# Transposing transfers in place of TensorE transposes for the first batch, with a new table of wanted times

## The chip, the cores and the metric

The kernel runs on one core of one Trainium2 chip. The metric is the device time of one execution in microseconds (us), taken as the median of several runs. The kernel before took 290.94 us (three runs, 290.71 to 290.95).

TensorE (PE in the profile; PEld is its weight load) multiplies matrices into PSUM, which has eight banks here. VectorE (DVE), ScalarE (ACT) and GpSimd (POOL) do elementwise work. Transfers are issued from the queues of SyncE (SP), POOL and ACT and run on 16 DMA engines. Each engine executes its own instructions in the order in which they were written; across engines an instruction waits on semaphores.

## The reference

Sort-net attention, followed by a Fourier mixing layer and an MLP, for 4 batches of 768 rows with 8 heads of 64:

```python
def _attn_ref(q, k, v, sort_net):
    ...                       # P: five rounds of row and column normalisation of exp(sort_net)
    k_sorted = np.einsum('bhij,bhjcd->bhicd', P, k_b).reshape(B, H, S, D)
    v_sorted = np.einsum('bhij,bhjcd->bhicd', P, v_b).reshape(B, H, S, D)
    ...                       # softmax attention inside blocks of 96 rows
    return np.matmul(attn, v_sb).reshape(B, H, S, D).astype(np.float32)

def _moe_ref(x, w_ch1, w_ch2):
    X = np.fft.fft(x, axis=1)
    X = np.fft.fft(X, axis=2)
    mixed = np.real(X).astype(np.float32)
    u = x + mixed
    mu = np.mean(u, axis=-1, keepdims=True)
    var = np.mean((u - mu) ** 2, axis=-1, keepdims=True)
    un = (u - mu) / np.sqrt(var + 1e-06)
    ch = np.maximum(un @ w_ch1, 0.0) @ w_ch2
    return (u + ch).astype(np.float32)
```

## The kernel before

**Stages.** Per batch `b`, `mix` multiplies k and v by the sort matrix (`k_mix`, L821; `v_mix`, L761, whose results DVE adds into the tile `vo`, L772, and `v_move` spreads to `vs` in twelve transfers from SP, L783). `q_mix` (L800) turns q. A step `psQK` is both L800 and L821 of one pair of heads. For each of four pairs of heads and two halves, `maxima` writes scores (`psS`, L853, 16 products for both halves of a pair) and DVE reduces them (`max`, L863); `scores` (`psT`, L875 then L853) gives the scores less their maxima to an exponential on ACT (L880), `minus_one` (L922 on ACT, L924 on DVE) writes the tile `eT`, and `values` (`psN`, L937) makes the attention output, which DVE normalises into `xr` (L943, L944). Batches 0 and 1 take this path; batches 2 and 3 a turned one (`turned`, L892 to L913). Then follow the sequence transform (`fold`, `dft_s`: L983, L995, L999, L1005), the feature transform (`dft_d`: L1035, L1039, L1045, whose results DVE combines as `PQ`, L1058), the residual (L1088; for batch 0 DVE adds in L1100 and L1101), the statistics (`stats`, L1115 and L1116), `root` (ACT, L1124 and L1125), `nm` (DVE, L1128) and `normal`, which writes a tile of normalised rows `un` [128 rows x 512] on ACT (L1138) or DVE (L1141). There are two `un` buffers.

**The turn.** `transpose_u` puts the tile `un[b, i, m]` into `unT` with features on the partitions. For batches 1 to 3 it is one transposing transfer from the SP queue (L1153). For batch 0 it is four TensorE transposes into a PSUM bank (L1162) and a copy from the bank to `unT` on ACT or DVE (L547). There are six such tiles in a batch, three to a group: group 0 is (i, m) = (0,0), (0,1), (1,1), group 1 the others. `mlp(b, gr)` multiplies a whole group: 64 products of L1180 (`ph`) into ACT's `relu` (L1186), then 48 products of L1198 (`pc`) and the output (L1207, stores L1215 and L1219).

**The order.** Engine queues are not written by hand. The class `Plan` holds every step with its possible engines and nominal durations, walks a nominal time line when the kernel is built, and at each turn emits the step that could start first; of those within `NEAR` ns of the first it takes the one with the lowest priority number. That number comes from the nominal length of what hangs on the step, plus `LEAD[name][b]` and `MOVE[name][(b, k)]` in thousands; `REL` gives earliest times for loads. `fill` puts unread products (L687, here called fills) into planned gaps of TensorE of at least 250 ns before `FILL_END`, as long as the planned activity in a window of 3413 ns is under `FILL_LOW`. So a new table rearranges all engines, also where no line of computation was edited.

## Time and profile before

| what | value |
|---|---|
| median of three runs | 290.94 us |
| the profiled execution | 291.53 us, of which the span from the first to the last instruction is 289.7 us |
| mean granted TensorE clock | 0.985 of full speed |
| TensorE transposes of batch 0 (L1162) | 24 products, first at 54.34 us |
| copies to `unT` on ACT (L547) | 6, mean 585 ns |
| transposing transfers of `un` (L1153) | 18, first at 108.0 us |
| fills (L687) | 8 |

Busy time is the time in which an engine had an instruction under way; the granted clock says how fast TensorE was allowed to run in a slice. A bracket at the end of a timeline row is the idle time before the instruction and what ended it. In the view of the chain each piece is what the next one waited for.

### The profile page before, as it was taken

How to read it: one execution, taken by the hardware profiler on the slowest of the kernel's cores; microseconds unless marked ns; L12 is line 12 of the kernel's file. 1: busy time of each engine (PE TensorE's matmuls, PEld its weight loads, DVE VectorE, ACT ScalarE, POOL GpSimd, SP SyncE). 2: the span in 40 equal slices, each digit the busy share in tenths (PEclk: the TensorE clock that was granted, in tenths of full speed). 3: DMA queues.
4: the chain of work that ended last, by engine and by line, in shares of the span. 5: the costliest groups of instructions: out<-in, count | busy, mean ns of one | idle time of the engine just before them, and what ended most of it. 6: DMA issues, size and time to landing. Idle time of an engine off the chain costs nothing.

```text
span 289.7 us, 6877 instructions
## 1 busy us (share of the span) xinstructions
PE 276.1 (95%) x2598; PEld 161.9 (56%) x2598; DVE 191.5 (66%) x435; ACT 183.8 (63%) x455; POOL 122.0 (42%) x190
## 2 busy tenths in 40 slices
PE   7899999689999999999999999999999999999993
PEld 2467766257765565445555576455645645645541
DVE  6749988978797897673679998987866572001011
ACT  2368976778894779746495679788725832712700
POOL 8473736314226789765833256230023641112010
PEclk9979999979999999999999999999999999999998
DMA  7998969998856876969935862553311025002002
GB/s 101 182 162 169 154 106 163 185 140 136 107 88 104 112 147 96 124 143 186 130 88 113 154 112 38 115 144 75 70 38 38 36 54 129 36 34 77 1 36 74
DMA packets 50847, 30.41 MB, mean 105 GB/s; under 512 B 25962, under 2 KB 48900, under 8 KB 50812
## 3 DMA queue, kind: packets, MB, share of 16 engines
q0 software_dynamic: 19040, 19.40, 40.6%
q1 hardware_dynamic: 31574, 10.28, 18.9%
q8 instruction: 20, 0.33, 0.5%
q10 hardware_dynamic: 200, 0.30, 0.4%
q14 instruction: 13, 0.11, 0.2%
HBM read 28.50 MB, written 6.29 MB: 120 GB/s over the span
## 4 chain that ended last, share of the span: by engine, by line
PE 78%; DVE 14%; DMA 3%; issue 2%; ACT 1%; DVEq 0%
PE bank L1180 29%; PE bank L1198 24%; PE bank L983 3%; PE bank L853 3%; PE bank L937 3%; DMA eT<-es 2%; PE bank L1088 2%; PE bank L875 2%; PE bank L821 2%; PE bank L761 2%; PE bank L1005 1%; PE bank L800 1%; DVE st L1115 1%; PE bank L1045 1%; DVE mxs L863 1%
## 5 line engine op out<-in xcount | busy, mean ns | idle before, releaser
L1198 PE MATMUL bank<-w2sb,hr 128*128 128x512 f16 x384 | 90.0, 379 | 0.0
L1180 PE MATMUL bank<-unT,w1sb 128*128 128x384 f16 x512 | 89.2, 329 | 0.0
L1186 ACT ACTIVATE hr<-bank 128x384 f16<-128x384 f32 x128 | 60.7, 495 | 38.7 <-PE bank L1180 37.9
L1180 PEld LDWEIGHTS <-w1sb 128*128 128x128 f16 x512 | 49.1, 99 | 32.2 <-issue 1.5
L1219 POOL DMA_INDIRECT out_dram<-outt,idx_sb x22 | 22.6, 1026 | 88.5 <-DVE outt L1207 70.0
L1198 PEld LDWEIGHTS <-hr 128*128 128x128 f16 x384 | 36.0, 98 | 38.2
L1207 DVE SCALAR_TENSOR_TENSOR outt<-u,bank 128x512 f32<-128x512 f32 x24 | 16.4, 682 | 41.8 <-PE bank L1198 41.8
L892 ACT ACTIVATE sm<-bank,mns 96x96 f32<-96x96 f32 x128 | 32.3, 352 | 2.4 <-DVE mns L898 2.0
L944 DVE TENSOR_TENSOR xr<-bank,rz 96x512 f16<-96x512 f32 x32 | 22.0, 686 | 1.1
L547 ACT CAST W<-bank 128x384 f16<-128x384 f32 (+1 forms) x38 | 12.8, 380 | 12.9 <-PE bank L983 8.5
L1115 DVE BATCH_NORM_STATS2 st<-u 128x6 f32<-128x512 f32 x24 | 16.4, 681 | 4.0 <-POOL u L1101 3.9
L863 DVE TENSOR_REDUCE mxs<-bank 96x8 f16<-96x768 f32 x16 | 14.5, 949 | 5.6 <-PE bank L853 5.5
L1100 POOL TENSOR_TENSOR u<-u,PQ 128x257 f32<-128x257 f32 x18 | 12.8, 711 | 9.9 <-DVE PQ L1058 8.6
L898 DVE TENSOR_REDUCE mns<-bank 96x8 f32<-96x768 f32 x16 | 15.0, 944 | 2.6 <-PE bank L853 2.2
L1101 POOL TENSOR_TENSOR u<-u,PQ 128x255 f32<-128x255 f32 x18 | 12.6, 699 | 3.6 <-DVE PQ L1058 3.6
L908 ACT ACTIVATE es<-sm 96x384 f16<-96x384 f32 x19 | 10.0, 528 | 6.1 <-DMA eT<-es 5.8
L880 ACT ACTIVATE sm<-bank 96x768 f32<-96x768 f32 x16 | 12.8, 801 | 1.4 <-PE bank L853 1.2
L922 ACT ACTIVATE eT<-sm 96x768 f16<-96x768 f32 x16 | 13.4, 841 | 0.4
L569 POOL DMA_DIRECT2D k<-in_k_dram x15 | 11.0, 733 | 5.9 <-PE bank L821 4.8
L937 PEld LDWEIGHTS <-eT 97*128 97x128 f16 (+1 forms) x256 | 11.2, 101 | 3.8 <-ACT eT L922 0.5
L943 DVE RECIPROCAL rz<-bank 96x8 f32<-96x8 f32 x32 | 6.3, 197 | 10.6 <-PE bank L937 10.5
L983 PE MATMUL bank<-cso_sb,xso 120*128 120x384 f16 (+1 forms) x64 | 13.1, 326 | 0.0
(144 smaller groups left out, 426.5 us busy)
## 6 DMA issues: line engine op xcount, KB each, us to landing
vs<-vo SPq DMA_DIRECT2D x48, 65.0 KB
v<-in_v_dram POOLq DMA_DIRECT2D x16, 192.0 KB, 4.9
k<-in_k_dram POOLq DMA_DIRECT2D x15, 192.0 KB, 5.5
q<-in_q_dram POOLq DMA_DIRECT2D x15, 192.0 KB, 4.1
w1sb<-in_moe_w_ch_dram POOLq DMA_DIRECT2D x4, 512.0 KB, 8.0
w2sb<-in_moe_w_ch_dram POOLq DMA_DIRECT2D x4, 512.0 KB, 5.9
eT<-es SPq DMA_TRANSPOSE x32
cdh_sb<-cdh SPq DMA_DIRECT2D x1, 387.0 KB
```

Source lines behind the costliest of these rows:

```text
L863: ("max", b, {"V": 945}, lambda e: nc.vector.tensor_reduce(mxs[n].t.rearrange("p (t j) -> p t j", t=2), pair(pS, BLK), axis=AX.X, op=ALU.max),
L892: nc.scalar.activation(sm.t[:, i], pair(pS, BLK)[:, t, i % 4], AF.Exp, bias=mn.t[:, i:i + 1], scale=-1.0)
L898: ("max", b, {"V": 945}, lambda e: nc.vector.tensor_reduce(mn.t.rearrange("p (t j) -> p t j", t=2), pair(pS, BLK), axis=AX.X, op=ALU.min), ...
L937: nc.tensor.matmul(ps[0:wide(i).stop - BLK * i, i // 4, i % 4], et[0:97, wide(i)], vs[b % 2][:, 4 * y + i % 4, (D + 1) * h:(D + 1) * (h + 1)])
L944: nc.vector.tensor_tensor(xr2[b % 2][0:BLK, 4 * y:4 * y + 4, 128 * hp:128 * hp + 128].rearrange("p j (t d) -> p t j d", t=2), ps[:, :, :, ...
L983: nc.tensor.matmul(ps, x[0:n, j], cso[0:n, j, :], start=(j == 0), stop=(j == 3))
L1115: nc.vector.bn_stats(st.t, us[b, i, m].t)
L1180: nc.tensor.matmul(ps, w1sb[:, mc, 128 * fc:128 * fc + 128], unT[b, gr].t[:, mc, :], start=(mc == 0), stop=(mc == 3))
L1186: nc.scalar.activation(dst, bank(pH, [128, 384]), AF.Relu)
L1198: nc.tensor.matmul(ps, hr[f4].t[:, fc % 4, 128 * t:128 * (t + 1)], w2sb[:, fc, :], start=(fc == 0), stop=(fc == 15))
L1207: step("outt", b, {"V": 687}, lambda e, u=u, pC=pC, o=o: nc.vector.scalar_tensor_tensor(o.t, u.t, RSC, bank(pC, [128, DM]), op0=ALU.mult, ...
L1219: step("store", b, {"G": 1050}, lambda e: nc.gpsimd.indirect_dma_start(out=out.rearrange("b s m -> (b s) m"), out_offset=bass.IndirectOffs ...
```

## The change

`transpose_u` takes the transfer for every batch, and the plan has other numbers: `FILL_LOW`, `FILL_END`, `NEAR`, `SPARE`, `REL`, `LEAD` and `MOVE`. In the changed file lines after L253 stand four lower (L1162 has become L1166, L1180 is L1184).

```diff
-    FILL_LOW, FILL_END, WINDOW = 1931, 49895, 3413
-    LAG, PE_TAIL, MARGIN, NEAR = 45.0, 250.0, 120.0, 14.0
+    FILL_LOW, FILL_END, WINDOW = 2169, 68436, 3413
+    LAG, PE_TAIL, MARGIN, NEAR = 45.0, 250.0, 120.0, 10.0
...
-    SPARE = 909
+    SPARE = 1004
...
-        un=(48.6, 33.2, -20.3, -21.5), unT=(0, 62.4, 0, 15.1),
+        un=(69.9, -4.9, 1.3, 0.6),
...
         dst = lambda: unT[b, gr].t[:, :, 128 * t:128 * t + 128]
-        if b:
+        if True:
             step("turn_u", b, {"S": 1310}, lambda e: nc.sync.dma_start(
                 dst(), un[b, i, m].t, transpose=True),
                 r=[un[b, i, m]], w=[(unT[b, gr], t)], work=850, hop=900)
```

What moves, counted from the two programs: the 24 products of L1162 and the six copies are gone, six transposing transfers stand on SP (24 instead of 18), and there are 23 fills instead of 8. Ahead of the first product of L1180, TensorE has three more `psQK` steps of batch 1 (four instead of one), three more `psT` of batch 1 (five instead of two), 48 more products of `psS` (64 instead of 16) and the four products of L713. Between the row of `psN` for the last `eT` of batch 0 and the first `psS` of batch 1 it has two more groups of L983, one more `psQK` and one fill less. On DVE, between the first `max` of batch 1 and the first L1180, there are two more `max` before the first `PQ`, two more adds of `vo` before `un` of tile (1,1), and one `minus_one` (L924), which was on ACT.

TensorE before, the end of the stretch that leads to the first product of the MLP (`kron` and `v16` belong to `v_mix`, `un` is a tile of normalised rows):

```order
L1162 LDWEIGHTS un0_138
L1162 MATMUL bank_65<-ident_153,un0_138 128x128
...
L761 LDWEIGHTS kron1_85
L761 MATMUL bank_65<-v161_77,kron1_85 128x384
L1180 LDWEIGHTS w1sb_185
L1180 MATMUL bank_65<-unT0_140,w1sb_185 128x384
```

TensorE now, the same place (`mxs2_92` is the maximum of a `psT` of batch 1, third pair of heads):

```order
L879 LDWEIGHTS mxs2_92
L879 MATMUL bank_65<-small_sb_149,mxs2_92 128x96
...
L857 LDWEIGHTS kz2_172
L857 MATMUL bank_65<-qT2_88,kz2_172 128x96
L1184 LDWEIGHTS w1sb_185
L1184 MATMUL bank_65<-unT0_140,w1sb_185 128x384
```

Before, the MLP's first product stood behind transposes and a product of `v_mix`; now it stands behind a `psT` that needs a maximum from DVE. In the run of L1184 that follows, 56 products stand without a break, where 8 stood before.

DVE now, the piece that holds the normalised rows of tile (1,1) (`u3_119`) and that maximum:

```order
L776 SCALAR_TENSOR_TENSOR vo_174<-a16_194,bank_65 128x6x64 x4
L1104 TENSOR_TENSOR u5_121<-bank_65,PQ0_114 128x257
L1105 TENSOR_TENSOR u5_121<-bank_65,PQ0_114 128x255
L1119 BN_STATS st2_131<-u5_121 128x6
L1120 BN_AGGR mv2_128<-st2_131 128x2
L1145 TENSOR_SCALAR un1_139<-u3_119,mv1_127,rstd1_133 128x512
L776 SCALAR_TENSOR_TENSOR vo_174<-a16_194,bank_65 128x6x64
L557 TENSOR_SCALAR kz3_173<-bank_65 128x768
L712 CAST amt_191<-bank_65 128x4x16
L713 TENSOR_TENSOR amt_191<-bank_65,amt_191 128x4x8
L867 TENSOR_REDUCE mxs2_92<-bank_65 96x8
```

Before, ACT wrote `un` of tile (1,1) and `kz` of this pair (L549); now both are DVE's, and seven of the eight adds of `vo` and all statistics of the batch stand ahead of them.

SP now, around the six new transfers (`vs1_176` is `vs` of batch 1):

```order
L748 DMA xr1_184<-a16_194 1x16x32
L1157 DMA_TRANSPOSE unT0_140<-un0_138 128x4x128
L1157 DMA_TRANSPOSE unT0_140<-un1_139 128x4x128
L787 DMA vs1_176<-vo_174 16x8x260 x4
L1157 DMA_TRANSPOSE unT0_140<-un1_139 128x4x128
L1157 DMA_TRANSPOSE unT1_141<-un0_138 128x4x128
L787 DMA vs1_176<-vo_174 16x8x260 x5
L1157 DMA_TRANSPOSE unT1_141<-un1_139 128x4x128
L1157 DMA_TRANSPOSE unT1_141<-un0_138 128x4x128
L787 DMA vs1_176<-vo_174 16x8x260 x3
```

Before, twelve transfers of `v_move` stood here in one run and no transposing transfer; now the third turn, the last that group 0 needs, stands behind four of them.

74 lines of the change are left out of this document (39 added, 35 removed).

## The prediction

> **What bounds the kernel now.** I read the page first, for the span and the chain that ended last.
>
> ```profile
> span 289.7 us, 6877 instructions
> ...
> PE 78%; DVE 14%; DMA 3%; issue 2%; ACT 1%; DVEq 0%
> ```
>
> TensorE carries most of the chain, so what counts is when TensorE cannot work and how much work it has left. The view in windows shows where that is (columns: the window, its length, busy time of PE, PEld, DVE, ACT and POOL with their instructions, granted TensorE clock, share of the DMA engines, GB/s).
>
> ```profile
> 50.00:60.00 10.00, 6.13 (x59) 3.69 (x58) 9.61 (x29) 7.02 (x16) 4.04 (x7) 0.96 1.06 161
> 60.00:70.00 10.00, 9.86 (x151) 6.60 (x150) 7.68 (x16) 7.74 (x15) 2.99 (x4) 0.87 0.89 133
> 100.00:110.00 10.00, 9.55 (x112) 5.95 (x111) 9.45 (x18) 8.35 (x24) 8.81 (x16) 1.00 0.83 146
> 120.00:130.00 10.00, 9.43 (x71) 4.61 (x70) 7.13 (x15) 5.16 (x18) 6.47 (x11) 1.00 0.71 141
> 54.80:58.20 3.40, 2.02 (x11) 0.82 (x11) 3.23 (x11) 3.37 (x8) 0.00 (x0) 1.00 1.26 199
> 59.30:62.70 3.40, 3.26 (x16) 1.70 (x14) 3.40 (x10) 2.32 (x4) 0.00 (x0) 0.52 0.83 112
> ```
>
> From 50 to 60 us TensorE is busy for 6.13 of 10 us while DVE is busy for 9.61: there DVE sets the pace. The two later windows that I show, with 9.55 and 9.43, are the only ones between 70 and 280 us that lose more than 0.1 us. So the time is the start of the first MLP product (L1180), plus the work that TensorE then has left, plus little. The narrow windows show that work too: with 2.02 of 3.40 us busy from 54.8 on, the granted clock in the window from 59.3 is 0.52. The chain tells what released the first L1180:
>
> ```profile
> 59.02 0.54 PE bank L1162 x4
> ...
> 60.70 2.27 PE bank L1180 x8
> 62.97 0.45 PE bank L1162 x8
> ```
>
> It started at 60.70 by the chain (60.49 by the timeline, which counts the pipelined start), behind transposes that themselves stood behind DVE.
>
> **The change, part by part.** Three things move: transposes and copies leave; work that stood behind the first L1180 now stands ahead of it; and the first L1180 itself moves.
>
> *Work that TensorE no longer has behind the first L1180.* Prices are differences of starts in the timeline (start, duration, engine, line, what):
>
> ```profile
> 44.65 0.51 PE L875 MATMUL bank<-small_sb,mxs 96*128 96x96 f16 x8
> ...
> 45.37 0.52 PE L875 MATMUL bank<-small_sb,mxs 96*128 96x96 f16 x8
> ...
> 60.49 2.47 PE L1180 MATMUL bank<-unT,w1sb 128*128 128x384 f16 x8
> 62.80 0.61 PE L1162 MATMUL bank<-ident,un 128*128 128x128 f16 x8
> ...
> 63.99 0.53 PE L800 MATMUL bank<-ident,q 128*64 128x128 f16 x12
> ...
> 65.45 0.40 PE L713 MATMUL bank<-ident,amt 128*128 128x128 f16 x4
> 65.69 0.81 PE L1180 MATMUL bank<-unT,w1sb 128*128 128x384 f16 x4
> 66.43 0.53 PE L800 MATMUL bank<-ident,q 128*64 128x128 f16 x12
> ...
> 67.23 0.52 PE L853 MATMUL bank<-kz,qT 64*128 64x96 f16 x16
> 67.67 1.47 PE L1180 MATMUL bank<-unT,w1sb 128*128 128x384 f16 x8
> ...
> 76.52 1.47 PE L1180 MATMUL bank<-unT,w1sb 128*128 128x384 f16 x8
> 77.82 0.51 PE L875 MATMUL bank<-small_sb,mxs 96*128 96x96 f16 x8
> ```
>
> The two transposed tiles behind it cost 0.45 (the chain's piece at 62.97; the other four tiles were ahead). Three psQK: 65.45 - 63.99 = 1.46 for two, 67.23 - 66.43 = 0.80 for the third, 2.26 together. L713: 65.69 - 65.45 = 0.24. Sixteen products of psS: 67.67 - 67.23 = 0.44; 48 are 1.32. A psT: 45.37 - 44.65 = 0.72; three are 2.16. Sum 6.43 us. So the break-even is simple: if the first L1180 starts 6.4 us later than 60.5, at 66.9, the end doesn't move.
>
> *When the first L1180 can start.* It now stands behind a psT that needs the maximum mxs2_92, and DVE has that behind all of the batch's statistics. The DVE rows of before:
>
> ```profile
> 43.46 1.82 DVE L863 TENSOR_REDUCE mxs<-bank 96x8 f16<-96x768 f32 x2 [0.99 <-PE bank L853]
> 45.20 0.75 DVE L1058 TENSOR_TENSOR PQ<-bank,ot 128x258 f32<-128x258 f32 x2
> 46.95 0.43 DVE L1100 TENSOR_TENSOR u<-bank,PQ 128x257 f32<-128x257 f32 x1 [1.00 <-PE bank L1088]
> ...
> 49.02 0.76 DVE L1058 TENSOR_TENSOR PQ<-bank,ot 128x258 f32<-128x258 f32 x2 [0.36 <-ACT ot L547]
> ...
> 58.41 1.49 DVE L772 SCALAR_TENSOR_TENSOR vo<-a,bank 128x384 f16<-128x384 f16 x3
> ...
> 60.81 0.54 DVE L1141 TENSOR_SCALAR un<-u,mv,rstd 128x512 f16<-128x512 f32 x1
> ...
> 62.66 0.22 DVE L708 CAST amt<-bank 128x64 f16<-128x64 f32 x1
> 62.91 0.19 DVE L709 TENSOR_TENSOR amt<-bank,amt 128x32 f16<-128x32 f32 x1
> ```
>
> The anchor is the first max of batch 1, at 43.46. It moves because TensorE has two more groups of L983, one more psQK and one fill less ahead of it:
>
> ```profile
> 42.49 0.65 PE bank L983 x4
> ...
> 48.27 0.65 PE bank L687 x3
> ```
>
> That is 2 x 0.65 + 0.80 - 0.22 = 1.88 at most. Part of it fills waits that TensorE has there, as the fills show: three fills' worth, 0.65, of the 1.88 I leave out and take 1.2; the ends are 0.6, where two thirds would be hidden, and 1.9. Then DVE in order:
>
> - four max instead of two: 45.20 - 43.46 = 1.74 for two, so 3.48;
> - from the first PQ to un, the same PQ, adds, statistics and five vo as before: 60.81 - 45.20 = 15.61, less the idle time in brackets, 1.00 and 0.36, which the two max ahead will cover: 14.25;
> - two more vo: 1.49 / 3 = 0.50 each with the overlap left in, say 0.95;
> - minus_one on DVE, which this trace doesn't have for a whole tile. Half a tile took 0.603 on DVE in the turned batches, and a tile of 128x768 out of PSUM 0.953:
>
> ```profile
> L910 DVE TENSOR_SCALAR es<-sm 96x384 f16<-96x384 f32 x13 | 7.8, 603 | 4.5 <-DMA eT<-es 2.6 <-ACT sm L892 1.5 <-ACT hr L1186 0.4
> ...
> L553 DVE TENSOR_SCALAR kz<-bank 128x768 f16<-128x768 f32 x3 | 2.9, 953 | 1.4 <-PE bank L821 1.4
> ```
>
> So between 0.6 (an operation for half the data) and 1.2 (two of them); I take 0.9, nearest to the row of the same width. ACT, which loses this step, is not waited for here.
>
> The normalised rows of tile (1,1) then start on DVE at 43.46 + 1.2 + 3.48 + 14.25 + 0.95 + 0.9 = 64.2. Two paths go on from there. On DVE: un 0.54, one vo 0.5, kz 0.95, the two small steps of amt 0.22 + 0.19, the max 0.91 (half of 1.82): 3.3, so 67.5; then the psT at 0.72, so 68.3. The other path is the transfer:
>
> ```profile
> 235.72 0.52 DVE L1141 TENSOR_SCALAR un<-u,mv,rstd 128x512 f16<-128x512 f32 x1
> ...
> 237.42 0.54 DVE L1141 TENSOR_SCALAR un<-u,mv,rstd 128x512 f16<-128x512 f32 x1
> ...
> 238.81 0.81 ACT L1138 ACTIVATE un<-u,nm,rstd 128x512 f16<-128x512 f32 x1 [2.44 <-DMA unT<-un]
> ...
> 241.91 0.55 DVE L1141 TENSOR_SCALAR un<-u,mv,rstd 128x512 f16<-128x512 f32 x1 [0.95 <-DMA unT<-un]
> ```
>
> In the last batch un ended at 235.72 + 0.52 = 236.24 and its buffer came free for ACT at 238.81: 2.57 us for a turn. The second, ended at 237.96, freed its buffer at 241.91: 3.95, with others queued ahead. With 2.57 the group is there at 64.2 + 0.5 + 2.6 = 67.3, hidden under the DVE path by 1.0; with 3.95 at 68.7, which would cost 0.4. On SP this turn is queued behind four v_move, whose vo stand on DVE ahead of three more vo and a tile's statistics; behind it wait the other v_move, and their vs is wanted only by psN, which now stands 56 products after the first L1184. POOL issues none of this.
>
> So the first L1180 comes at 68.3, 7.8 us later, against 6.4 us that it leaves behind: **1.4 us slower**. The ends: with 0.6 for the anchor and 0.6 for minus_one it is 67.4 (0.5 slower); with 1.9, 1.2 and the longer turn 64.2 + 0.7 + 0.3 + 0.5 + 3.95 = 69.7 (2.8 slower).
>
> *The fills.* Fifteen more at 0.22 would be 3.3 us, and I cost them at nothing: they stand where TensorE waits for DVE anyway (eight of them around psV and the psQK behind it, which wait for PSUM banks that DVE frees). If DVE were not late, they would be the whole loss.
>
> *The copies.* Six on ACT leave; ACT was not what the first L1180 waits for now, so nothing.
>
> *The clock.* Eight L1180 took 62.80 - 60.49 = 2.31 under the low clock and 77.82 - 76.52 = 1.30 at full speed: 1.0 us is lost today. In the change TensorE is again waiting for DVE between 55 and 68, with 23 fills in all, so I leave this loss as it is. It could vanish (-1.0), or a whole slow window of 3.4 us could fall on the products (1.7 instead of 1.0, +0.7).
>
> The Trainium skill (TensorE: Matmul & The Clock Gate, Part 1, What's actually happening) says that the array falls to half clock after an idle window of about 3.4 us and comes back after a busy one. The trace agrees on the half and on the length (0.52 over 3.4 us), but not on idle: 2.02 of 3.40 busy was not enough. By the rule, fills alone would keep the clock and the sum would be 0.4 us slower; by the row, 1.4.
>
> *Around the rest.* Everything after the first L1180 is re-ordered too, but the end is the same: the last two MLP groups run as whole blocks in both programs. The windows with 9.55 and 9.43 lose 1.0 us together; the new order may lose none of it or as much again. I take no difference, and 1.0 either way for the range.
>
> The profiled execution took 291.53 with a span of 289.7, 1.8 outside. Span 291.1, profiled 292.9; the median of the runs lies 0.59 under that execution, so **292.3**.
>
> **Rivals.**
>
> *The clock and the later stalls pay.* The fills keep the array above what the gate asks for, all 1.0 us comes back, the stream runs clean for another 1.0, and the chain is at its short end: 0.5 - 1.0 - 1.0 = -1.5, 289.4. It decides in favour of faster once the first L1184 starts before 67 with a clock of 1.0 in the window after it. For it: 15 more fills in just that stretch, and DVE is freed of two max, which before stood behind the first L1180. Against it: fills stand at planned gaps, and the wait for psV's banks is where the array is emptiest.
>
> *It balances.* The chain at its short end and half of the clock: 0.5 - 0.5 = 0, 290.9. For it: 7.8 against 6.4 are two big numbers each known to half a microsecond.
>
> *The turn becomes the bound.* The DMA share is 1.26 in the window from 54.8: the third turn, behind transfers of v and weights, takes 3.95 plus as long as an earlier one needs to clear (1.4 more). Then the group lands at 64.2 + 0.5 + 5.4 = 70.1 and with the longer anchor (0.7) at 70.8: 10.3 - 6.4 = 3.9 slower, 294.8. Against it: SP has nothing else queued there. The Trainium skill (VectorE: DVE Perf Modes, The three transpose paths and Rules for kernel authors) speaks for this side: TensorE where PSUM will do as target, 390 ns for 128x128, and 1309 ns by transfer. Its figure for four blocks one after the other would be an estimate of 5.2 us a tile and 3.3 us lost; the row of 2.57 us does not bear that out.
>
> *The change does not do what it says.* Of the 24 transposes 16 stood in a stretch where TensorE waited for DVE. Taking those away gives nothing, in any of the cases; only the 0.45 behind the first L1180 counts, and it is in the sum.
>
> **How the numbers follow.** The forecast, slower by 0.6 to 2.8, has 0.44. The turn as bound, or new stalls of that size, 0.16. Balance 0.15. Faster 0.25. About 0.2% (0.6 us) is what a measurement of this kernel can tell from no change. So faster 0.25, same 0.15, slower 0.60. The forecast's own range is 291.5 to 293.7. To leave out no more than 2 in 10, the range goes down to 290.0, most of the way to the fast case, and up to 294.5, just short of the turn as bound.
>
> **What would show it.** In the profile after: the first L1184 near 68.3, with 67 as the point that decides; DVE without idle from the first max of batch 1 (near 44.7) to mxs2_92; un of tile (1,1) near 64.2 and its turn about 2.6 us behind; TensorE idle or in fills for some 8 us between 54 and 68; the clock under 0.6 in a window that touches the first L1184; fewer than 1.5 us idle from there to the last product. The prediction is wrong in its mechanism if L1184 starts before 66 or is released by the transfer rather than by the psT, and wrong in its balance if the work behind it has not shrunk by 6.4 us.

## The result

| | before | after |
|---|---|---|
| median of the runs | 290.94 us | 300.08 us (298.12 to 301.91, four runs) |
| the profiled execution | 291.53 us, span 289.7 | 298.77 us, span 296.8 |
| mean granted TensorE clock | 0.985 | 0.980 |
| first L1180, now L1184 | 60.49 us | 73.60 us |

The ratio is 1.031 (95% interval 1.024 to 1.038): slower by 9 us, where 1.4 were forecast. Ratios leave out runs that lie far above their kernel's shortest (the profiled executions of e10 and e11 below are two such) and, for the experiments, the profiled execution; medians keep them all, so the two can differ.

The page of the changed kernel, span and chain:

```profile
span 296.8 us, 6876 instructions
...
PE 79%; DVE 8%; DMA 8%; issue 2%; POOL 1%; SPq 1%; ACT 0%; DVEq 0%; POOLq 0%
```

DMA has 8% of the chain, where it had 3%: transfers have become something that TensorE waits for. The chain names two of the pieces (start, length, what):

```profile
28.03 7.64 DMA cse_sb<-cse
...
77.80 5.96 DMA vs<-vo
```

The second is a `v_move` of batch 1, behind the start of the MLP. The first is the load of the constant `cse`, which stands nowhere in the prediction. TensorE's timeline shows what it did:

```profile
35.72 0.99 PE L999 MATMUL bank<-cse_sb,xse 120*128 120x386 f16 x3 [2.37 <-DMA cse_sb<-cse]
37.01 0.32 PE L1003 MATMUL bank<-nse,xse 96*128 96x192 f16 x1 [0.30 <-POOL nse L1337]
...
40.55 0.67 PE L941 MATMUL bank<-vs,eT 97*128 97x65 f16 x8
...
47.48 0.69 PE L857 MATMUL bank<-kz,qT 64*128 64x96 f16 x24
```

L999 and L1003 are the first products of the sequence transform of batch 0, and need `cse` and `nse`, which POOL makes of it. TensorE stood for 2.4 us, and its clock was at half from 35.50 to 42.33. The last `psN` of batch 0 (L941) came at 40.55, where it had been at 38.28:

```profile
38.28 0.43 PE L937 MATMUL bank<-vs,eT 97*128 97x65 f16 x8 [0.39 <-ACT eT L922]
```

The first `psS` of batch 1 followed at 47.48, where it was at 43.08 before. SP's timeline shows that `cse`, issued at 16.86 before, now stands behind eight `v_move` transfers (the last two rows are `v_move` of batch 1 and the turns of group 0's third tile and the next):

```profile
18.42 5.72 SPq L787 DMA_DIRECT2D vs<-vo  x6
...
26.73 1.26 SPq L787 DMA_DIRECT2D vs<-vo  x2
28.03 0.71 SPq L1247 DMA_DIRECT2D cse_sb<-cse  x1
...
66.32 2.55 SPq L787 DMA_DIRECT2D vs<-vo  x4
68.96 2.70 SPq L1157 DMA_TRANSPOSE unT<-un  x2
```

And POOL's shows what ran beside it. Before, the first quarter of `w2` (512 KB) came at 58.51. Now one comes at 26.14, as soon as the quarter of `w1` under way has landed, with k and v behind it:

```profile
25.90 0.18 POOL L497 COPY landed<-w1sb 1x1 f16<-1x1 f16 x1 [8.18 <-DMA w1sb<-in_moe_w_ch_dram]
26.14 0.75 POOL L1240 DMA_DIRECT2D w2sb<-in_moe_w_ch_dram  x1
...
28.95 0.74 POOL L573 DMA_DIRECT2D k<-in_k_dram  x1
29.69 0.72 POOL L563 DMA_DIRECT2D v<-in_v_dram  x1
35.77 1.18 POOL L1337 TENSOR_SCALAR nse<-cse_sb 96x384 f16<-96x384 f16 x1 [5.36 <-DMA cse_sb<-cse]
```

From there the DVE rows follow the forecast closely, and then fall behind once more:

```profile
47.94 3.55 DVE L867 TENSOR_REDUCE mxs<-bank 96x8 f16<-96x768 f32 x4 [1.48 <-PE bank L857]
...
55.05 0.84 DVE L928 TENSOR_SCALAR eT<-sm 96x768 f16<-96x768 f32 x1
...
68.28 0.52 DVE L1145 TENSOR_SCALAR un<-u,mv,rstd 128x512 f16<-128x512 f32 x1
...
69.80 0.96 DVE L557 TENSOR_SCALAR kz<-bank 128x768 f16<-128x768 f32 x1 [0.55 <-PE bank L825]
...
71.03 1.81 DVE L867 TENSOR_REDUCE mxs<-bank 96x8 f16<-96x768 f32 x2
```

The work between the anchor (the first max, 47.94) and `un` of tile (1,1) took 20.3 us. The last stretch, on TensorE:

```profile
66.38 1.89 PE L691 MATMUL bank<-junk 128*128 128x512 f16 x4
...
72.03 0.38 PE L717 MATMUL bank<-ident,amt 128*128 128x128 f16 x4 [0.51 <-DVE mxs L867]
72.25 0.59 PE L691 MATMUL bank<-junk 128*128 128x512 f16 x2
72.89 0.50 PE L879 MATMUL bank<-small_sb,mxs 96*128 96x96 f16 x8
...
73.60 6.67 PE L1184 MATMUL bank<-unT,w1sb 128*128 128x384 f16 x40
```

Four planned fills took 1.9 us at half clock (66.22 to 69.63), and behind the max (71.03) stand the four products of L717 (the step `psB`), two fills and the `psT` before the first L1184.

### The profile page after: what moved, and what is told of

Same layout as the page of the kernel before. It is cut to its first block, busy times and chain, and to the rows that moved or that the text cites. A ratio compares the mean times of both kernels' runs of the same rounds, so it can differ in the third digit from the quotient of the medians.

```text
span 296.8 us, 6876 instructions
## 1 busy us (share of the span) xinstructions
PE 279.9 (94%) x2589; PEld 163.5 (55%) x2589; DVE 188.9 (64%) x439; ACT 182.9 (62%) x445; POOL 121.7 (41%) x190
## 4 chain that ended last, share of the span: by engine, by line
PE 79%; DVE 8%; DMA 8%; issue 2%; POOL 1%; SPq 1%; ACT 0%; DVEq 0%; POOLq 0%
PE bank L1202 26%; PE bank L1184 26%; PE bank L987 3%; PE bank L857 3%; PE bank L1092 3%; DMA cse_sb<-cse 3%; PE bank L804 2%; PE bank L941 2%; DMA vs<-vo 2%; PE bank L825 2%; DMA q<-in_q_dram 2%; PE bank L1049 2%; PE bank L765 2%; PE bank L879 1%; PE bank L691 1%
## 5 line engine op out<-in xcount | busy, mean ns | idle before, releaser
L1202 PE MATMUL bank<-w2sb,hr 128*128 128x512 f16 x384 | 89.0, 379 | 0.0
L1184 PE MATMUL bank<-unT,w1sb 128*128 128x384 f16 x512 | 87.7, 326 | 0.0
L1184 PEld LDWEIGHTS <-w1sb 128*128 128x128 f16 x512 | 48.8, 98 | 32.2 <-issue 0.2
L551 ACT CAST W<-bank 128x384 f16<-128x384 f32 (+1 forms) x32 | 11.3, 388 | 18.2 <-PE bank L1009 7.4
L941 PEld LDWEIGHTS <-eT 97*128 97x128 f16 (+1 forms) x256 | 12.1, 106 | 4.9 <-issue 1.6
L941 PE MATMUL bank<-vs,eT 97*128 97x65 f16 (+1 forms) x256 | 13.2, 202 | 1.2 <-DMA vs<-vo 1.0
L553 ACT ACTIVATE kz<-bank 128x768 f16<-128x768 f32 x13 | 10.2, 812 | 5.4 <-PE bank L825 5.2
L926 ACT ACTIVATE eT<-sm 96x768 f16<-96x768 f32 x15 | 12.5, 842 | 1.3 <-PE bank L941 0.9
L585 POOL TENSOR_TENSOR vh<-v 128x384 f32<-128x384 f16 x12 | 11.2, 930 | 4.2 <-DMA v<-in_v_dram 2.3
```

Source lines behind the costliest of these rows:

```text
L941: nc.tensor.matmul(ps[0:wide(i).stop - BLK * i, i // 4, i % 4], et[0:97, wide(i)], vs[b % 2][:, 4 * y + i % 4, (D + 1) * h:(D + 1) * (h + 1)])
L1184: nc.tensor.matmul(ps, w1sb[:, mc, 128 * fc:128 * fc + 128], unT[b, gr].t[:, mc, :], start=(mc == 0), stop=(mc == 3))
L1202: nc.tensor.matmul(ps, hr[f4].t[:, fc % 4, 128 * t:128 * (t + 1)], w2sb[:, fc, :], start=(fc == 0), stop=(fc == 15))
```

## The experiments

All experiments but two keep every instruction of one of the two kernels, in its order on each engine, except for the pieces shown. The steps are recorded as the planner lays them out and written down at the end with those pieces moved, so lines of the experiments stand some lines lower than those above, and names are what to go by. "psS" is the start of the first `psS` of batch 1, "first MLP" that of the first L1180 or L1184, "half clock" the sum of the windows at half clock ahead of 280 us, all three of the profiled execution. The kernel before, run again beside the experiments, had medians of 291.2 to 292.0 us; ratios go by those runs. `psN`, `psT`, `psB` and `psV` (the products of L761) name TensorE's part of a step.

| run | median us (lowest to highest) | ratio to before (95%) | psS | first MLP | half clock |
|---|---|---|---|---|---|
| before | 290.9 | | 43.08 | 60.49 | 6.8 |
| after | 300.08 (298.1 to 301.9) | 1.031 (1.024 to 1.038) | 47.48 | 73.60 | 10.2 |
| e1, cse early | 298.23 (298.0 to 299.7) | 1.024 (1.016 to 1.032) | 47.62 | 74.21 | 13.7 |
| e3, w2 late | 299.02 (297.0 to 300.9) | 1.027 (1.017 to 1.038) | 46.23 | 72.81 | 6.8 |
| e4, both | 300.36 (297.2 to 301.6) | 1.031 (1.023 to 1.040) | 46.59 | 72.67 | 6.8 |
| e5, before, turn only | 299.05 (296.0 to 299.9) | 1.022 (1.012 to 1.032) | 43.06 | 65.51 | 17.1 |
| e8, cse early, w2 much later | 296.26 (294.9 to 297.6) | 1.013 (1.005 to 1.021) | 47.00 | 73.82 | 10.2 |
| e2, before, cse late | 297.82 (296.5 to 298.6) | 1.019 (1.010 to 1.027) | 48.83 | 66.30 | 17.1 |
| e10, before, w2 early | 294.13 (289.7 to 296.0) | 1.002 (0.996 to 1.009) | 45.25 | 62.42 | 10.2 |
| e9, before, half the turns | 293.62 (291.0 to 298.4) | 1.004 (0.999 to 1.009) | 41.93 | 59.09 | 6.8 |
| e11, after, fills | 298.89 (296.4 to 301.9) | 1.024 (1.016 to 1.031) | 49.60 | 76.97 | 13.7 |
| e15, e2 with fills | 296.04 (294.5 to 297.6) | 1.018 (1.012 to 1.025) | 46.03 | 63.19 | 3.4 |
| e12, e5 with fills | 299.21 (295.4 to 301.1) | 1.030 (1.022 to 1.037) | 41.47 | 65.42 | 3.4 |
| e13, e8 with fills | 296.89 (296.1 to 300.8) | 1.018 (1.013 to 1.022) | 44.44 | 72.74 | 10.2 |
| e16, before, loads beside a turn | 291.80 (290.4 to 293.9) | 1.001 (0.996 to 1.006) | 42.45 | 59.72 | 6.8 |
| e17, e8 and more | 299.54 (297.8 to 300.4) | 1.025 (1.017 to 1.033) | 44.26 | 72.64 | 10.2 |
| e18, after, six fills less | 300.63 (300.0 to 301.3) | 1.029 (1.022 to 1.037) | 48.70 | 74.64 | 20.5 |
| e19, before, short products | 293.38 (291.3 to 295.3) | 1.007 (1.003 to 1.011) | 43.04 | 60.20 | 0 |

### Undoing the new places of cse and w2 (e1, e3, e4)

```diff
 SP, batch 0 (e1, e4):
+DMA cse_sb<-cse
 DMA vs<-vo x6
 DMA xr<-m x3
 DMA vs<-vo x2
-DMA cse_sb<-cse
 DMA vs<-vo x4
 POOL (e3, e4):
-COPY landed<-w1sb
-DMA w2sb<-in_moe_w_ch_dram
 TENSOR_TENSOR kron x2
 DMA k
 DMA v
 TENSOR_SCALAR nse<-cse_sb
+COPY landed<-w1sb
+DMA w2sb<-in_moe_w_ch_dram
```

> The changed kernel, with one instruction moved: the load of cse stands on SP ahead of the v_move transfers of batch 0, as it did before, instead of behind eight of them. Theory A (the late load of cse and the slow clock that the wait brings make the loss beyond the forecast): TensorE no longer waits for cse at 35.7 us, the granted clock stays near 1.0 between 36 and 42 us, the first psS of batch 1 comes at 43 to 44.5 instead of 47.5, the first L1184 3 to 4.5 us earlier than 73.6, and the time falls by 3 to 5 us, to 294 to 297. Rival B (the transposing transfers are what costs): the wait at 35.7 goes, but the time falls by less than 1 us. Rival C (the new order of DVE in batch 1 decides the first L1184): the first psS comes earlier, the first L1184 by less than half of that, and the time falls by 1 to 2 us.

> The changed kernel, with one load moved: the quarter of w2 that POOL issued at 26.1 us (behind a wait for w1) stands behind nse instead. cse is issued where the changed kernel has it, at 28 us. Theory A1 (the load of cse is slow because 512 KB of w2 run beside it, and nse waits behind it on POOL): cse lands in 3 to 4 us instead of 7.6, near 31.5, TensorE hardly waits, and the time falls by 3 to 5 us as in the kernel with the early cse. Theory A2 (being issued at 28 is late enough by itself): cse lands near 34 or later and the time falls by less than 1.5 us. Rival B: less than 1 us whatever cse does.

> The changed kernel with both moves: cse ahead of the v_move transfers and the quarter of w2 behind nse. Theory A: about the time of the kernel with the early cse alone (within 1 us), 294 to 297, since either removes the same wait; still 3 to 6 us slower than before, because the first L1184 stands behind DVE by the rest (68 to 70 us, against 66.9 that would balance). Rival B: 297 to 299.

Theory A missed in all three: 1.9, 1.1 and -0.3 us instead of 3 to 5, and the intervals overlap that of the changed kernel. The wait for `cse` went (in e3 it shrank from 2.4 to 0.6 us), but TensorE's row in e1 shows a new one 1.6 us further on, and e1's chain names it:

```profile
37.36 1.56 PE L956 MATMUL bank<-vs,eT 97*128 97x65 f16 x24 [2.28 <-DMA vs<-vo]
```

```profile
30.33 6.90 DMA vs<-vo
```

The last `v_move` of batch 0, issued at 30.33, landed 6.9 us later, and the first `psS` came no earlier than before the edit. In e4 the same wait took 2.7 us: there `nse` no longer holds POOL up, so `w2` comes at 30 us and does the same harm. In e3 TensorE waited 1.6 us for the load of q instead, which was now behind `w2` on POOL. In these profiles one late transfer hid the next.

### The turn alone (e5)

```diff
-            ps = bank(pY, [128, 4, 128], F16)
-            for c in range(4):
-                nc.tensor.matmul(ps[:, c], un[b, i, m].t[:, 128 * c:128 * (c + 1)], ident, is_transpose=True)
+            nc.sync.dma_start(dst(), un[b, i, m].t, transpose=True)
...
-                   ("unT", b, {"A": 585, "V": 400}, lambda e: copy(
-                       e, dst(), bank(pY, [128, 4, 128], F16)), [pY], [(unT[b, gr], t)]))
+                   ("unT", b, {"A": 585, "V": 400}, lambda e: None, [pY], [(unT[b, gr], t)]))
```

> The kernel before, in its own order, with nothing but the turn changed: the four TensorE transposes and the copy of each of the six tiles of batch 0 are replaced, at the place of the transposes, by a transposing transfer from SP. Theory A (the turn by transfer is about as fast as TensorE with its bank and copy where TensorE waits for DVE anyway): the first L1180 within 0.7 us of 60.5, the time within 1 us of before, 290 to 292. Rival B (the transfers are what costs): each group of the MLP waits 2.6 us or more for its third tile, the time rises by 2 to 5 us, 293 to 296.

Rival B held in kind, and the loss was above its 2 to 5 us: 2.2% slower (299.05 us against 291.85 of the kernel before beside it), with nothing else moved. The rows of the turns on SP, of `un` on ACT and of the first L1180 (here L1188):

```profile
54.30 2.62 SPq L1171 DMA_TRANSPOSE unT<-un  x2
...
62.94 2.60 SPq L1171 DMA_TRANSPOSE unT<-un  x2
```

```profile
53.46 1.52 ACT L1149 ACTIVATE un<-u,nm,rstd 128x512 f16<-128x512 f32 x2 [0.52 <-DVE nm L1139]
...
61.39 1.52 ACT L1149 ACTIVATE un<-u,nm,rstd 128x512 f16<-128x512 f32 x2 [5.51 <-DMA unT<-un]
```

```profile
65.51 4.00 PE L1188 MATMUL bank<-unT,w1sb 128*128 128x384 f16 x12 [6.02 <-DMA unT<-un]
```

The first two tiles were written by 54.98 us and their turns issued from 54.30 on, but the next writers of the two buffers ran only at 61.39: 7 us for turns that I had put at 2.57. The third turn, issued at 62.94, let the MLP start at 65.51, and the first twelve products ran at half clock, which lasted from 54.21 to 71.28. What stood in the way is in the view of the DMA queues (queue, packets, MB, share of 16 engines) for 50 to 58 us:

```profile
q0 software_dynamic: 1696, 1.51, 119.3%
q14 instruction: 1, 0.01, 0.3%
```

q0 carries POOL's loads and q1 SP's transfers. POOL's loads of k and `w1` have a share of over 100%, and of q1 there is not one packet, though SP has issued two turns from 54.30 on and the first of three small transfers at 57.02. In before and after together there are 111 microseconds in which POOL's loads have a share of 1.0 or more; in those SP's queue has a mean share of 0.015 and at most 0.24. That figure doesn't say in how many of them SP had anything to send.

### Both loads out of the way, and the opposite edits on before (e8, e2, e10, e9)

e8 is e1 with the quarter of `w2` moved behind the last loads of q and v for batch 1. e2 puts `cse` and `nse` of the kernel before where the changed one has them, e10 the quarter of `w2`. In e9 only the second group's three tiles are turned by transfers (the edit of e5 behind `if gr:`).

> The changed kernel with two loads moved: cse ahead of the v_move transfers (as in the run with the early cse), and the quarter of w2 that POOL issued at 26.1 us much later on POOL, behind the last loads of q and v for batch 1. Theory S (while POOL's loads fill the DMA engines, a transfer from SP gets next to nothing, so whatever SP sent last before such a load lands late: cse in the changed kernel, v_move in the run with the early cse): the last v_move of batch 0 lands by 34 us instead of 37.2, no idle stretch of TensorE over 1 us between 30 and 44, the first psS of batch 1 at 43.5 to 45 instead of 47.5, the first L1184 near 70.5, and the time falls by 2 to 4 us, to 295 to 297. Rival O (the new order behind the first psS decides, and what is won ahead of it is lost there, as in the three runs before): the first psS comes earlier and the time falls by less than 1 us.

> The kernel before, in its own order, with the load of cse moved to where the changed kernel has it, behind eight v_move transfers, and nse on POOL behind the second load of v. POOL has no load of weights near it here. Theory S (lateness on SP costs nothing by itself, a large POOL load beside it does): cse is issued near 27.5 us, lands within 3.5 us, L995 still starts within 0.7 us of 32.6, and the time is within 0.8 us of before. Rival L (the place behind the v_move transfers is what costs): cse lands after 34 us, TensorE waits 2 us or more, and the time rises by 2 to 4 us.

> The kernel before, in its own order, with one load moved: a quarter of w2 (512 KB) is issued by POOL near 26 us, behind a wait for the quarter of w1 that is under way, where the changed kernel has it, instead of near 66. cse stays early. Theory S: the SP transfers that are under way from 27 to 31 us (v_move, cso) land 3 us or more later than before, TensorE waits 1.5 us or more between 29 and 40, and the time rises by 1.5 to 4 us. Rival L (the load is harmless, only the order on SP counts): the time within 0.7 us of before.

> The kernel before, in its own order, with only the second group of three tiles of batch 0 turned by transfers from SP; the first group keeps TensorE and its copies. Theory S (a turn by transfer costs where the MLP waits for it while loads are under way, and nothing where there is slack): the first L1180 within 0.5 us of 60.5, TensorE has 0.2 to 0.5 us less work behind it, the time between 0.7 us less and 0.7 us more than before. Rival T (the transfers of batch 0 cost by themselves, through SP's queue or the un buffers): 2 us or more slower.

e8 is the one edit that brought the changed kernel back by a measured amount, 3.8 us, inside the range of theory S. But the steps that the theory named did not come in its profile: TensorE still waited 1.2 us for `v_move`, the first `psS` came at 47.00 instead of 43.5 to 45, and the first MLP product no earlier than before the edit. What released that product is no longer the psT:

```profile
36.01 0.93 PE L960 MATMUL bank<-vs,eT 97*128 97x65 f16 x24 [1.21 <-DMA vs<-vo]
...
73.82 1.46 PE L1203 MATMUL bank<-unT,w1sb 128*128 128x384 f16 x8 [0.80 <-DMA unT<-un]
```

It waited 0.80 us for `unT`: the turn was next in line. The profiled execution is the longest of the four, 297.57 us at a mean granted clock of 0.979; the other three ran at 0.991 and 0.992. So where the 3.8 us were won is not shown. e2 went against theory S and for rival L: `cse`, issued at 29.96 us, landed 4 us later, TensorE waited twice (1.5 us for `v_move`, 1.2 ahead of the product that needs `cse`), half clock lasted from 30.63 to 44.28, and the time rose by 5.9 us against the kernel before beside it, though only a load of v (192 KB) was near. POOL's row of `nse` shows the landing:

```profile
33.94 1.18 POOL L1351 TENSOR_SCALAR nse<-cse_sb 96x384 f16<-96x384 f16 x1 [6.40 <-DMA cse_sb<-cse]
```

So standing behind `v_move` costs with a small load near it too; that it would cost with none is not shown.

e10 can't be decided: the profiled execution, which the ratio leaves out, has psS 2.2 us later, and the ratio shows no change. e9 held: where the MLP has slack, a turn by transfer costs nothing that can be measured.

### Is it the clock? (e11, e15, e12, e13)

All kernels showed half clock behind these waits. Four kernels got fills where TensorE only waits.

```diff
 TensorE (e11: x10; e15: x7; e13: none)
+MATMUL bank<-junk
 MATMUL bank<-cse_sb,xse
 TensorE (e15: x5, first psN; e13: x7, fifth psN)
+MATMUL bank<-junk
 MATMUL bank<-vs,eT
 TensorE (e12: x25, x6 and x5 more ahead of it)
+MATMUL bank<-junk
 MATMUL bank<-unT,w1sb
 TensorE, last psQK of batch 1 (e11, e13: x5 more)
+MATMUL bank<-junk
 MATMUL bank<-ident,q
```

> The changed kernel, all its instructions in their order, with fills added where TensorE only waits: ten ahead of the first psWe (the wait for cse, 2.4 us) and five more beside those ahead of the last psQK of batch 1 (a wait of 1.7 us for DVE). Theory G (the waits themselves are the smaller part; a window of 3.4 us in which TensorE is busy for less than about 2.1 us is followed by half clock, and that is the larger part): the wait for cse stays, no window of half clock begins between 34 and 60 us, the first psS of batch 1 comes 1.5 to 3 us earlier than 47.5, and the time falls by 2 to 4 us from 300.1, to 296 to 298. Rival W (the waits are the loss, the clock only follows them): the time falls by less than 1 us, or rises by what the fills cost (up to 3 us).

> The kernel before with the late cse (the run that took 297.8, with TensorE waiting for 3 us in all between 29 and 36 us and 13.7 us of half clock behind it), with five fills ahead of the first psN and seven ahead of the first psWe, where it waits. Theory G: no window of half clock between 28 and 50 us, the time back to 292 to 294.5. Rival W: the time stays at 296.5 to 298.5.

> The kernel before with only the turn changed (the run that took 299.05, with TensorE waiting 6.0 us for the third turn and 17 us of half clock), with fills where it waits: five ahead of L695 of batch 1, six among the places of the old transposes, 25 ahead of the first L1180. Theory G: the first L1180 still comes at 64.5 to 66 us, since the turn is as late as it was, but the clock stays high, and the time falls by 2.5 to 4.5 us, to 294.5 to 296.5; what is left against before, 3 to 5 us, is the wait for the transfer itself. Rival W: the time stays at 298 to 300, or above where the fills overrun the wait.

> The changed kernel with the early cse and the late quarter of w2 (the run that took 296.3), with fills where it still waits: seven ahead of the psN that waits for v_move at 36 us, and five more ahead of the last psQK of batch 1. Theory G: no half clock between 34 and 60 us, at most one window of it between 60 and 72, the first psS at 44 to 45.5 us, the time 293 to 295, which is near the forecast for the change (292.3). Rival W: the time stays at 295.5 to 297.5.

In the profiled executions of e15 and e12 the half clock shrank from 17.1 to 3.4 us, and these two took 294.48 and 295.39 us. The medians moved less: 1.8 us less for e15, 0.2 more for e12, 1.2 less for e11, 0.6 more for e13, against 2 to 5 expected. By the times theory G missed.

Two things keep this from settling what the clock is worth. First, the profiles bear the theory out as far as the first `psS`. e13 has the orders of e8 with fills added: its waiting psN came 0.4 us later (36.43, in e8 36.01), and its first `psS` still 2.6 us earlier (44.44 against 47.00), inside the range of the theory, without the half clock that e8 had from 37.40 to 44.23. e15 has it 2.8 us earlier than e2. What e13 won it lost again: five extra fills came to stand behind the wait that they were meant for, and nine fills took 4 us at half clock. The same five stand there in e11. In e12 the first L1180 stands right behind the last fill, so the wait itself can't be read from it.

Second, half clock differs from one execution of a program to the next. e12's other three ran at mean granted clocks of 0.986, 0.973 and 0.980 instead of 0.994, so the half clock was back in them. e13 took 296.06 us at 0.994 and 299.77 at 0.981, e11 296.39 at 1.00 and 300.08 at 0.980. Of 56 comparable executions of the kernel before, 35 had a clock of 0.99 or more and a mean time of 291.1 us, the others a lower one and 292.5. Whether the clock makes the difference, or a late transfer makes both, is not shown.

### A load beside a turn, and the crossed kernels (e16, e6, e7)

```diff
 POOL, batch 3 (e16):
 TENSOR_TENSOR u<-u,PQ x2
+DMA k<-in_k_dram x3
 DMA out_dram<-outt,idx_sb
```

> The kernel before, in its own order, with three loads of 192 KB from POOL added near 234 us, beside the transposing transfers of the last batch, where no load runs otherwise. They fetch again what the buffers of k already hold, and nothing reads it. The turn of the second tile (from the end of un to the next writer of its buffer) took 2.57 us without them. Theory S (SP's transfers get next to nothing while POOL's loads fill the DMA engines): it takes 4.5 us or more, and the packets of the SP queue come in the gaps of the loads; the time rises by up to 3 us, as far as the first L1180 at 243.5 waits. Rival F (the engines are shared fairly, the late turns of batch 0 have another reason): it takes at most 3.5 us and the time stays within 0.7 us.

> The changed kernel's table of wanted times with the turn of batch 0 still by TensorE, its bank and its copies. The planner lays out its own order for it, which is neither of the two. Theory S (the loss has two parts, the table's places for cse and w2, about 4 us, and the transfers themselves under the loads of that stretch, about as much): 293 to 297. Rival T (only the transfers cost): within 1 us of before. Rival N (the new table is the whole loss): 298 to 301.

> The kernel before with its own table and the turn of batch 0 by transfers; the planner lays out its own order for it. cse stays early and no w2 is near it. Theory S: the turns wait for the loads of w1 and k that POOL sends between 47 and 53 us, the first L1180 comes at 64 us or later, and the time is 295 to 299. Rival N: within 1 us of before.

e16 measured the disputed cost by itself, far from the change. `un` of the second tile and the next writer of its buffer:

```profile
236.84 0.79 DVE L1155 TENSOR_SCALAR un<-u,mv,rstd 128x512 f16<-128x512 f32 x1
...
242.99 0.81 ACT L1152 ACTIVATE un<-u,nm,rstd 128x512 f16<-128x512 f32 x1 [5.49 <-DMA unT<-un]
```

From 237.63 to 242.99: 5.36 us for the turn, 2.57 without the loads. In the view of the queues for 237 to 240 us SP's queue has two packets:

```profile
q0 software_dynamic: 598, 0.43, 111.4%
q1 hardware_dynamic: 2, 0.00, 0.1%
```

Theory S held, and the time didn't move: the next MLP group started at 244.64 without a wait. The crossed kernels say nothing on the parts: 309.96 us (306.5 to 314.0) and 303.25 us (301.9 to 305.6, ratio 1.039, 1.031 to 1.048), both slower than either kernel and outside every expectation. The planner laid out a new order for each mixture, and both orders were worse.

### Everything at once, and the clock on before (e17, e18, e19)

e17 is e8 with seven fills ahead of the waiting psN, 16 and 28 short unread products (128x128) in the waits between the psV of batch 1, and without the six planned fills ahead of the last psQK and of the psT; e18 is the changed kernel without those six; e19 is before with 4 and 20 short products between the psV.

> The changed kernel with all that the runs so far point to: cse early, the quarter of w2 late, seven fills ahead of the psN that waits for v_move, the six planned fills ahead of the last psQK and of the psT before the first L1184 taken out (four of them took 1.9 us at half clock and held up kz), and 44 short unread products in the two waits of TensorE for DVE between the psV of batch 1, written to the free end of their banks. Theory G (late transfers, then half clock, then fills on the path, and nothing else, lie between forecast and result): no half clock between 34 and 72 us, the first psS near 44.5, un of tile (1,1) near 65, the first L1184 at 68.5 to 70 (the forecast was 68.3), the time 292 to 294.5. Rival O (the new order behind the first psS is slow by itself): the first L1184 at 71.5 or later and the time 295.5 or more.

> The changed kernel without the six planned fills ahead of the last psQK and of the psT that stands before the first L1184. Theory P (those fills stood on the path: 1.9 us of them at half clock ahead of kz, 0.4 us ahead of psT): DVE no longer waits for kz, the first L1184 comes 0.8 to 1.5 us earlier after un of tile (1,1) (5.3 us in the changed kernel), and the time falls by 0.5 to 1.5 us from 300.1. Rival N (fills cost nothing, as the prediction has it): the distance from un to the first L1184 within 0.3 us of 5.3 and the time within 0.5 us.

> The kernel before, with 24 short unread products in TensorE's waits between the psV of batch 1 (55 to 59 us, busy for 1.45 of 3.41 us there), written to the free end of their banks. Theory G (half clock follows a window in which TensorE is busy for less than about 2.1 of 3.4 us): the window of half clock at 59.1 goes, eight L1180 take 1.3 to 1.6 us instead of 2.31, and the time falls by 0.3 to 1.2 us against before. Rival W: the clock window stays or the short products hold TensorE up, and the time is within 0.5 us of before or above it.

In e17 the anchor came back: psS at 44.26, the first max at 44.71. The first MLP product still came at 72.64, and time and place are those of rival O. The chain and TensorE's row name the reason, and POOL's row what ran beside it:

```profile
66.54 5.97 DMA unT<-un
```

```profile
72.64 3.68 PE L1228 MATMUL bank<-unT,w1sb 128*128 128x384 f16 x11 [1.43 <-DMA unT<-un]
```

```profile
62.45 0.74 POOL L1284 DMA_DIRECT2D w2sb<-in_moe_w_ch_dram  x1
```

The turn of tile (1,1) was issued at 66.54 behind four `v_move`, and landed 6.0 us later: 512 KB of `w2` filled the engines until 67.5, and SP's queue had the `v_move` to move first. In this order a better anchor does not bring the transfer in before 72.5. From 67.31 to 77.55 the clock was at half as well. e18 shows that the six fills cost nothing on balance: from `un` of tile (1,1) to the first L1184 it took 5.14 us, with them 5.32, and the time didn't fall; rival N held. They were not idle weight, though. The wait for kz went, as theory P had it, but without the fills half clock lasted from 65.12 to 78.77, where it had been 66.22 to 69.63, and TensorE's steps there took longer (the first eight products of the psT 0.80 us instead of 0.50).

In e19's profile the half clock at 59.1 is gone and eight L1180 take 61.49 - 60.20 = 1.29 us, where they took 2.31:

```profile
57.52 1.28 PE L473 MATMUL bank<-junk 128*128 128x128 f16 x20
58.98 0.85 PE L1181 MATMUL bank<-ident,un 128*128 128x128 f16 x8 [0.18 <-DVE vo L791]
...
60.20 1.46 PE L1199 MATMUL bank<-unT,w1sb 128*128 128x384 f16 x8
61.49 0.61 PE L1181 MATMUL bank<-ident,un 128*128 128x128 f16 x8
```

TensorE was 1.2 us ahead there, and by 125.8 us, at a product that waits 0.77 us for ACT, the lead was gone. So in this execution the won window was worth nothing at the end. The time rose by 0.7% (0.3 to 1.1), but that ratio says little on the clock: only the profiled execution ran at 0.997, and the mean of the twelve, 0.990, is that of the kernel before beside it. No version was measurably faster than the kernel before.

## Why the prediction was wrong

The direction was right (slower, 0.60), the time was not: 300.08 lies 5.6 us above the range. By steps, with the last rows of both kernels for the ends of the MLP:

```profile
274.68 10.52 PE L1198 MATMUL bank<-w2sb,hr 128*128 128x512 f16 x48
```

```profile
281.72 10.52 PE L1202 MATMUL bank<-w2sb,hr 128*128 128x512 f16 x48
```

| step | forecast | measured |
|---|---|---|
| work behind the first MLP product | 6.43 less | (285.20 - 60.49) - (292.24 - 73.60) = 6.07 less |
| first max of batch 1 | 44.7 | 47.94 |
| from there to `un` of tile (1,1) | 19.5 | 20.34 |
| from there to the first L1184 | 4.1 | 5.32 |
| span | 291.1 | 296.8 |

- **The balance** was right: 6.07 against 6.43, and the span is longer by the 5.3 us by which the first L1184 is later than forecast, plus 0.4. As a law it isn't: in e13, e17 and e19 a better start of the MLP was lost again behind it.
- **The anchor** is the first step that failed, and the largest, 3.2 of the 5.3 us: "It moves because TensorE has two more groups of L983, one more psQK and one fill less ahead of it". The list of what moved was read on TensorE and DVE, and on SP only around the turns. That `cse` had gone behind eight `v_move` on SP, and a quarter of `w2` ahead of it on POOL, was not priced, nor was a clock that falls ahead of the MLP. In the changed kernel TensorE waited 2.4 us for `cse`, ran at half clock to 42.33, and had the last `psN` of batch 0 at 40.55 instead of 38.28. With both loads moved away and fills in the wait (e13 and e17) the first max is at 44.89 and 44.71, so the sum over TensorE held, at its upper end: in e13 it takes 6.60 us from that `psN` (37.84) to the first `psS`, 1.80 more than before, where 1.88 was the most. With the loads moved and no fills (e8) the max is at 47.46. The 3.2 us are therefore the late transfers and the half clock behind them together, and the profiles do not divide them.
- **The transfer path** is the second: "With 2.57 the group is there at 64.2 + 0.5 + 2.6 = 67.3, hidden under the DVE path by 1.0". The 2.57 came from the last batch, where POOL loads nothing beside that turn. Beside loads a turn took 5.4 (e16), 6.0 (e17) and 7 us (e5). In the changed kernel this is hidden by the late psT; as soon as that comes earlier, the turn decides (e8, e17). The rival "the turn becomes the bound" had the mechanism, with "behind transfers of v and weights" as its cause, and was given a sixth of the chance and 294.8 us; its argument against, "SP has nothing else queued there", looked at the wrong queue.
- **The other rivals**: no start ahead of 67 and no balance came. That taking the transposes away gives nothing but the 0.45 us in the sum fits the balance.
- **The new steps on DVE** were right: four max 3.55 (forecast 3.48), `minus_one` 0.84 (0.9). The 0.84 more up to `un` are waits for TensorE's banks (0.52 and 0.31 for L1092). The 1.2 more behind it are DVE's wait for kz (0.55) and the psB and two fills ahead of the psT.
- **The fills** cost nothing on balance, as forecast, but for another reason than forecast: they held the clock (e18).
- **The clock** was priced at the MLP's products alone. Half clock rose from 6.8 to 10.2 us and lies ahead of the MLP now (full clock from 69.6 on), where it helped to make the anchor late. What a window of it is worth in time stays open. The window that the prediction read, 2.02 us busy from 54.8 on, was off the grid on which the clock changes; on it, 55.71 to 59.12 has 1.45 us busy, and half clock follows at 59.12.
- **Two smaller points.** The 3.3 us in the rival of the turn come out as 3.1 from its own rows. And 0.2% was taken as what a measurement can tell; the intervals here reach 0.4% to 1.0% either way.
- **The median** lies 1.3 us above the profiled execution, where it lay 0.6 below before: 1.9 of the 7.8 us.

What divides the 9 us: the places of `cse` and `w2` are worth 1.8 points of the 3.1% (e8), by the time and not by a row of the profile, and what is left, 1.3%, holds the forecast 0.5% and what else the new order costs, the late turn among it. e2 and e5 alone cost 1.9% and 2.2%, together more than the whole; that late transfers cover one another, as in e1, would explain it, but is not shown for these two. How the last 1.3% divides is not settled: e17, meant to settle it, brought 44 new products with it, had half clock under the first MLP products, and its time was above that of e8.

## What to carry to other kernels

A transfer's duration depends on its place as much as on the transfer: take it from a row with the same other queue loading beside it, and read the packets of each queue in that window before calling a transfer hidden. When an order is laid out anew, list every issue on every queue that changed sides with another, constants and weights too, not only those around the edit. And when undoing one late transfer brings nothing, look for the next one behind it before dropping the theory. Compare the granted clock of every execution, not of the profiled one alone, before saying what the clock is worth.

## What the hardware showed that was not expected

**SP's transfers can stand still beside POOL's loads.** In e16 SP's queue had two packets in 3 us in which POOL's was at 111.4%, and in e5 none in the 3.7 us from the issue of the first turn to 58 us, in a stretch in which POOL's was at 119.3%. The Trainium skill (DMA: Bandwidth & Descriptors, Queues, rings and completion order) says that each engine takes turns between the queues that have work, a packet at a time. By that a turn beside loads would be slowed, not stopped; in these two windows it was stopped. It is no rule for all transfers: in the changed kernel SP's queue had no packet from 28 to 31 us, while `cse` and `v_move` waited and POOL's had 98.9%, but from 33 to 35 us both moved, at 41.4% and 85.7%. What decides between the two is not shown.

**Half clock follows a window that is two fifths idle.** Windows of the changed kernel, on the grid on which the clock changes:

```profile
32.09:35.50 3.41, 1.27 (x19) 0.77 (x17) 1.38 (x3) 3.02 (x4) 0.00 (x0) 1.00 1.20 214
35.50:38.91 3.41, 2.89 (x16) 1.91 (x16) 0.63 (x2) 0.00 (x0) 2.67 (x3) 0.50 1.07 233
38.91:42.32 3.41, 3.41 (x38) 2.49 (x36) 2.78 (x8) 1.37 (x3) 2.74 (x5) 0.50 0.92 171
```

1.27 of 3.41 us busy was enough for half clock, and it lasted for a second window though the first was busy for 2.89. Over all 20 profiles, the windows at full clock from 8 us on: of 32 with less than 1.99 us busy 31 were followed by half clock, of 16 between 1.99 and 2.30 two, of over 1500 above that one. The two limits were drawn from these same windows. The Trainium skill (TensorE: Matmul & The Clock Gate, Part 1, What's actually happening) gives the window's length, 3413 ns, and the trace agrees; it speaks of an idle window, and the trace does not.
